# Decay attention and sticky mixture of experts: early outputs scaled on GpSimd, and a new order beside the early tiles

## The chip, the cores and the metric

One core of a Trainium2 chip runs the whole kernel. The metric is the device time of one execution in microseconds. TensorE does the matmuls, VectorE and ScalarE take results out of PSUM, GpSimd (POOL) splits weights and issues the indirect transfers, and SyncE (SP) issues all the other transfers. Each engine works off its own instructions in the order in which they were written; engines wait for each other through semaphores.

## The reference

The first half is causal attention with a decay, for 8 batches of 8 heads, 576 positions and 64 columns a head. Its output, with the heads side by side, is `x` with 512 columns a token. The second half is a mixture of 8 experts in which a token may keep the expert of the token before it:

```python
logits = np.einsum('bsd,de->bse', x, w_gate)
local_gate = 1.0 / (1.0 + np.exp(-np.einsum('bsd,de->bse', x, w_local).squeeze(-1)))
...
            fresh_e = int(np.argmax(logits[b, s]))
            if s == 0 or local_gate[b, s] < 0.5:
                e = fresh_e
            else:
                e = prev_e if prev_e >= 0 else fresh_e
...
            h = np.maximum(x[b, s] @ w1[e], 0.0)
            out[b, s] = p[e] * (h @ w2[e])
```

`p` is the softmax of the token's logits, so each output row is multiplied by one probability. `w1[e]` is 512 by 1024 and `w2[e]` 1024 by 512.

## The kernel before

Attention runs batch by batch. All values that matter are kept as a high and a low float16 part, so that a product is three matmuls (high by high, high by low, low by high). The tokens go to DRAM (`xs`), to be gathered by expert later.

Routing (`route`, L1352) is done for pairs of batches, four times. It has a critical part (`crit`: `mxs`, `fresh`, `gated`, `rows`, ... `place`, `place2`, `slot`, `marks`, `invert`, `invert2`) that finds each token's slot, and a part that isn't needed at once (`rest`: `prob`, `prob2`, `prob3`, `prob4`, `pmarks`, `pinvert`, `pinvert2`) that brings the probabilities into the same slots. Most steps are small VectorE operations. Some are small matmuls into `psG`, a pool of one PSUM bank (L1797), so the next such matmul may be issued only when the last result has been read.

After the third pair, the tokens of the first six batches are known. So three tiles of 128 tokens each, for experts 0 and 1, can be computed at once (`both_early`, L1994), while the last two batches are still being routed. Expert 0's weights `W0` and the first two of eight blocks of expert 1's (`PW`, `NP = 2`) are split into high and low by GpSimd; the other six blocks of expert 1 are split by `piece` (L2010): the high part by ScalarE (L1822), the low one by VectorE (L1826), and the load of a later block behind it.

`experts` (L1655) is a generator. In the first layer it takes eight chunks `fc` of 12 matmuls into `z` (two PSUM buffers). The relu of a chunk, a ScalarE instruction to `hh` and a VectorE one to `hl`, is issued after the matmuls of the next chunk. Then it takes three tiles of 24 matmuls into `y` (two buffers); `put` of a tile (L1671), a ScalarE copy to `o` that multiplies by the probability and a scatter by GpSimd, is issued after the matmuls of the next tile. For the early tiles, `experts` yields after every two matmuls: expert 0 has the steps 0 to 47 (first layer) and 48 to 83 (second), expert 1 the steps 84 to 131 and 132 to 167.

`run` (L1719) goes through these steps and calls what is due at each: `todo` and `at` are two lists, sorted by step. `AT` (L63) holds the steps of the last pair's critical routing; `beside(x, f)` (L1900) adds `f` at step x. This table alone decides what stands in an engine's line ahead of a relu. At the same step, functions are called in the order in which they were added.

What is added by name: `turn_xl` turns the last tokens of the last batch; `mult`, `half`, `add` (from `gate`) make the last batch's logits from `xt`; `close_attention` (L1848) frees attention's memory, opens the pools for expert 1's weights and starts their loads; `late_tok` (L1873) gathers expert 0's late tokens and `next_tokens` (L1876) expert 1's (`x1l`), each gather being followed by a transpose on SyncE, with three buffers `xg`; `totals`, `ranks`, `numbers`, `rank_loads` prepare the other experts, which are taken in the order of their load; `early_probs` gives the probabilities of the early tiles.

Then `fixed` (L2133) computes the late tiles of experts 0 and 1, and `ranked` those of the other six.

Of the kernel before, what the change touches and what calls it, by code (L numbers as in the profile page):

```python
# [59 lines left out]
HB = (1, 1)  # L60
ST = 4
XP = 20
AT = (6, 15, 18, 30, 30, 36, 44, 49, 62)  # L63

T0 = 9700.0
DUE = (("k2", 11000), ("q2", 12500), ("k3", 14500), ("q3", 15500), ("v", 18000), ("v4", 20500), ("a", 26000), ("b", 29000))
# [6 lines left out]
def kernel(  # L73
# [1116 lines left out]
    def whole(fn):  # L1190

        for _ in fn() or ():
            pass
# [91 lines left out]
    def rtile(shape, dt, name):  # L1285
        return rt.tile(shape, dt, name=name)
# [65 lines left out]
    def route(g, last):  # L1352
# [4 lines left out]
        OH = OHA[:, g]  # L1357
        R = {}
        NV = nc.vector
        aux, AUX = (nc.gpsimd, POOL) if big is nc.gpsimd else (NV, None)  # L1360

        def mxs():
            R["mx"] = rtile([128, GC], F32, "mx")
            R["kp"] = rtile([128, 2, GC], F16, "kp")
            NV.tensor_reduce(R["mx"], Lx, axis=AX.X, op=ALU.max)
            yield
            NV.scalar_tensor_tensor(R["kp"], Lg[:, :, E].unsqueeze(1).broadcast_to([128, 2, GC]), ZTHR, notfirst,
                                    ALU.is_gt, ALU.mult)
            R["mxb"] = R["mx"].unsqueeze(2).broadcast_to([128, GC, E])
# [110 lines left out]
            aux.tensor_tensor(hm, t128[:, gs], ov, ALU.add)  # L1480

        def marks():
            HI = R["HI"] = rtile([128, GC, NM], F16, "HI")
            RH = R["RH"] = rtile([128, GC, 2, NM], F16, "RH")
            LO = R["LO"] = rtile([128, GC, 128], F16, "LO")
            NV.tensor_tensor(HI, imain.unsqueeze(1).broadcast_to([128, GC, NM]),
                              R["hm"].unsqueeze(2).broadcast_to([128, GC, NM]), ALU.is_equal)
            yield 320 if big is NV else 1480
            if big is NV:
                NV.tensor_scalar(RH[:, :, 0], HI, irow[:, 0:1], None, ALU.mult)  # L1490
                yield 250
                NV.tensor_scalar(RH[:, 4::5, 0], HI[:, 4::5], irow[:, 1:2], None, ALU.mult)
                yield 2060
            else:
                big.tensor_scalar(RH[:, :, 0], HI, irow[:, 0:1], 1.0, ALU.mult, ALU.mult)
                big.tensor_scalar(RH[:, 4::5, 0], HI[:, 4::5], irow[:, 1:2], 1.0, ALU.mult, ALU.mult)
            big.tensor_tensor(RH[:, :, 1], HI, icol[:, gs].unsqueeze(2).broadcast_to([128, GC, NM]), ALU.mult)
            NV.tensor_tensor(LO, i128.unsqueeze(1).broadcast_to([128, GC, 128]),
                              lo[:, gs].unsqueeze(2).broadcast_to([128, GC, 128]), ALU.is_equal)
# [145 lines left out]
    def tokens(pool, xT, cols, n, rows=NT, half=False):  # L1645
# [6 lines left out]
            nc.sync.dma_start_transpose(out=xT[:, :, i * 128:i * 128 + m], in_=xg[0:m])  # L1652
        return xT

    def experts(W, xT, n, prob, scat, hp, op, width=704, every=6, half=None):  # L1655

        wh, wl, uh, ul = W
# [11 lines left out]
            nc.vector.scalar_tensor_tensor(lv, z[:, 0:nh, 0:wd], 0.0, hv, ALU.max, ALU.subtract)  # L1669

        def put(t, y):  # L1671
            o = op.tile([128, DM], F32, name="o", bufs=2 if op is ep else 3)
            nc.scalar.activation(o, y, AF.Copy, scale=prob(t))  # L1673
            nc.gpsimd.indirect_dma_start(out=outf, out_offset=bass.IndirectOffsetOnAxis(ap=scat(t), axis=0), in_=o,  # L1674
                                         in_offset=None, bounds_check=NT - 1, oob_is_err=False)
# [172 lines left out]
    def close_attention():  # L1848
# [3 lines left out]
        EX["wpb"] = ctx.enter_context(tc.tile_pool(name="wpb", bufs=1))  # L1852
        EX["W"] = wtiles(EX["wpb"])
        stage2 = EX["stage"] = ctx.enter_context(tc.tile_pool(name="stage2", bufs=ST))

        first = early_weights(stage2, EX["W"], range(NP), 1)
        for _, f in first[0:2]:
# [18 lines left out]
    def next_tokens(cols, n2, rows=NT):  # L1876
        return tokens(EX["xp"], EX["xp"].tile([128, 8, 704], F16, name="xT"), cols, n2 // 2, rows, bool(n2 % 2))
# [12 lines left out]
    def both(*fs):  # L1890
        return lambda: [whole(f) for f in fs]
# [1 line left out]


    last = gate(B - 1)
    todo = [turn_xl, lambda: whole(last[0]), both(*last[1:], close_attention, *crit[0:3]), both(*crit[3:6]), both(*crit[6:8]), both(*crit[8:10]),
            both(*crit[10:13]), both(*crit[13:17]), both(*crit[17:19], all_idx, late_tok)]
    at = list(AT)

    def beside(x, *fs):  # L1900

        at.append(x)
        todo.append(both(*fs))
# [107 lines left out]
        NW.pop(0)()  # L2011

    for i in range(4 * NP):
        beside(19 + 3 * i, lambda: EX["PW"].pop(0)())
    REST = EX["rest"]
    for x, f in zip((0, 1, 2, 3, 4, 34, 35), REST, strict=True):
        beside(x, f)
    beside(36, early_probs)
    beside(19, open_ranks)
    beside(64, lambda: EX.update(x1l=next_tokens(lambda i: EX["ga"][:, CAP + EARLY + i:CAP + EARLY + i + 1], CAP2[1] - 2 * EARLY)))  # L2020
    for i in range(16 - 2 * NP):
        beside(65 + 24 * i // (16 - 2 * NP), piece)
    for i, f in enumerate((totals, ranks, numbers, rank_loads, gathers, *rest, all_probs, scatters, half_tiles, caps)):
        beside((63, 63, 64, 95, 96)[i] if i < 5 else 92 + 6 * (i - 5), f)
    seq = sorted(range(len(at)), key=lambda x: at[x])
    run(both_early(), [todo[x] for x in seq], [at[x] for x in seq], 400)
    pump(0)
    sidx, xp_, wpb = EX["sa"], EX["xp"], EX["wpb"]
    ectx.close()

# [223 lines left out]
```

## Time and profile before

| | |
|---|---|
| median of 3 runs | 891.14 us (891.06 to 893.96) |
| the profiled execution | 888.74 us, span 887.0 us |
| mean granted TensorE clock | 0.964 |
| TensorE busy | 784.8 us, 88% |
| VectorE busy | 525.2 us, 59% |
| ScalarE busy | 433.3 us, 49% |
| GpSimd busy | 404.9 us, 46% |
| attention's last matmuls | near 434.8 us |
| early tiles | 434.9 to 531.6 us |

In the rows of the timeline, the first number is the start in us from the span's start, the second the duration of the group, then engine, line, operation, output and inputs, shapes and count. What stands in brackets at the end is how long the engine sat idle just before, and what ended that. A row with "x2" or "x3" stands for instructions back to back. `PEclk` in the tables of stretches is the granted clock of TensorE as a share of its full speed.

### The profile page before, as it was taken

What the parts mean: (1) busy time and instruction counts of PE and PEld (TensorE: products, weight loads), DVE (VectorE), ACT (ScalarE), POOL (GpSimd) and SP (SyncE); (2) the same over time, 40 slices, a digit from 0 to 9 for tenths busy, and PEclk for the clock granted to TensorE, in tenths of its full rate; (3) what the DMA queues carried; (4) which work ended last, traced back from release to release, by engine and by line L of the source; (5) the groups of instructions that cost most, each with busy time, mean ns of one, the idle gap of its engine ahead of it and who ended that gap; (6) DMA issues with size and microseconds to landing.
All of it is one profiled execution on the core that took longest, in us unless ns stands there. A gap on an engine that the chain in (4) does not pass through costs nothing. (4 is left out here: it accounts for less than half of the span.)

```text
span 887.0 us, 20948 instructions
## 1 busy us (share of the span) xinstructions
PE 784.8 (88%) x8438; PEld 542.5 (61%) x8438; DVE 525.2 (59%) x1120; ACT 433.3 (49%) x804; POOL 404.9 (46%) x473
## 2 busy tenths in 40 slices
PE   5776999889997898969769498999999999999993
PEld 3655778667876787757534256575564847575541
DVE  8765878888878877888857331534073634434110
ACT  4764778758876687748413111534142424323110
POOL 9595768487854969236981200321311212121100
PEclk9988999999999999989979799999999999999997
DMA  6979979586974868079472800657354654735000
GB/s 164 190 132 222 180 166 171 118 172 142 156 171 83 159 137 164 4 157 216 100 264 60 272 24 25 153 184 204 113 146 164 151 176 147 193 123 143 37 16 29
DMA packets 205588, 124.81 MB, mean 141 GB/s; under 512 B 145612, under 2 KB 181582, under 8 KB 205404
## 3 DMA queue, kind: packets, MB, share of 16 engines
q1 hardware_dynamic: 199345, 104.04, 51.4%
q0 software_dynamic: 6144, 19.41, 6.7%
q8 instruction: 67, 1.10, 0.5%
q14 instruction: 32, 0.26, 0.1%
HBM read 72.41 MB, written 19.62 MB: 104 GB/s over the span
## 5 line engine op out<-in xcount | busy, mean ns | idle before, releaser
L1682 PE MATMUL z<-xT,wh 128*128 128x288 f16 (+4 forms) x960 | 186.0, 305 | 26.9 <-DVE hl L1669 26.9
L910 ACT ACTIVATE P<-st,nm 128x512 f32<-128x512 f32 (+3 forms) x288 | 152.4, 585 | 39.7 <-DVE nm L890 35.5
L890 DVE TENSOR_REDUCE nm<-st 128x1 f32<-128x512 f32 (+4 forms) x264 | 134.5, 544 | 28.5 <-PE st L886 17.4
L1669 DVE SCALAR_TENSOR_TENSOR hl<-z,hh 128x576 f16<-128x576 f32 (+5 forms) x80 | 52.7, 663 | 164.7 <-ACT hh L1668 164.5
L930 ACT CAST ph<-pt 128x512 f16<-128x512 f32 (+1 forms) x200 | 115.7, 582 | 55.4 <-PE pt L925 54.0
L925 PE MATMUL pt<-ident,P 128*128 128x128 f32 x784 | 125.0, 284 | 14.9 <-DVE pl L934 7.9
L1682 PEld LDWEIGHTS <-wh 128*128 128x128 f16 x960 | 94.0, 99 | 68.8 <-issue 20.0
L934 DVE TENSOR_TENSOR pl<-pt,ph 128x512 f16<-128x512 f32 x168 | 111.8, 669 | 27.6 <-ACT ph L930 25.5
L1682 PE MATMUL z<-xT,wl 128*128 128x288 f16 (+4 forms) x480 | 120.2, 305 | 0.0
L1704 PE MATMUL y<-ul,hh 128*128 128x512 f16 x288 | 109.2, 379 | 0.0
L1704 PE MATMUL y<-uh,hl 128*128 128x512 f16 x288 | 109.2, 379 | 0.0
L1704 PE MATMUL y<-uh,hh 128*128 128x512 f16 x288 | 109.1, 379 | 0.0
L1668 ACT ACTIVATE hh<-z 128x576 f16<-128x576 f32 (+5 forms) x80 | 45.9, 575 | 124.4 <-PE z L1682 121.2
L925 PEld LDWEIGHTS pt<-ident,P 128*128 128x128 f32 x784 | 85.9, 144 | 32.4 <-issue 9.7
L1704 PEld LDWEIGHTS <-hh 128*128 128x128 f16 x576 | 56.2, 98 | 65.6
L904 PE MATMUL xp<-VH,pl 128*128 128x65 f16 (+1 forms) x960 | 91.6, 195 | 4.3 <-DVE pl L934 4.3
L1674 POOL DMA_INDIRECT out_dram<-o,ranki x26 | 27.3, 1049 | 147.4 <-ACT o L1673 116.8
L904 PE MATMUL xp<-VH,ph 128*128 128x65 f16 (+1 forms) x960 | 93.5, 197 | 0.9 <-ACT ph L930 0.9
L904 PE MATMUL xp<-VL,ph 128*128 128x65 f16 (+1 forms) x960 | 92.4, 195 | 0.0
L879 PE MATMUL st<-KB,QB 70*128 70x256 f16 (+4 forms) x448 | 80.4, 290 | 13.1 <-DMA KB<-Ak 8.5
L904 PEld LDWEIGHTS <-ph 128*128 128x128 f16 (+1 forms) x1920 | 84.1, 103 | 8.7 <-issue 3.3
L879 PE MATMUL st<-Ak,Aq 128*128 128x256 f16 (+4 forms) x448 | 80.9, 293 | 7.6 <-ACT P L910 7.2
(378 smaller groups left out, 1295.5 us busy)
## 6 DMA issues: line engine op xcount, KB each, us to landing
stg<-in_moe_w_dram SPq DMA_DIRECT2D x64, 512.0 KB
xs<-xr SPq DMA_DIRECT2D x16, 512.0 KB
ldq<-in_q_dram SPq DMA_DIRECT2D x14, 512.0 KB
ldk<-in_k_dram SPq DMA_DIRECT2D x14, 512.0 KB
ldv<-in_v_dram SPq DMA_DIRECT2D x28, 256.0 KB
KB<-Ak SPq DMA_DIRECT2D x14, 256.0 KB
QB<-Aq SPq DMA_DIRECT2D x13, 256.0 KB
ldv<-in_v_dram SPq DMA_DIRECT2D x20, 64.0 KB
```

The costliest lines, as they stand in the source:

```text
L879: nc.tensor.matmul(st[p0:p0 + m, co:co + n], lhsT=queries(lq, kk, h, c), rhs=rhs, start=(ps == 0 and first and co == col), stop=(ps == 1), ...
L890: nc.vector.tensor_reduce(dst, src, axis=AX.X, op=ALU.max, negate=True)
L904: nc.tensor.matmul(xo, lhsT=a[:, c0:c0 + m], rhs=w[:, vi, :], start=False, stop=(i == n - 1 and jj == 2), skip_group_check=True)
L910: nc.scalar.activation(P[:, c0:c1].rearrange("p (k x r) -> p k r x", r=2, x=64), st[:, c0:c1].rearrange("p (k r x) -> p k r x", r=2, x=64) ...
L925: nc.tensor.matmul(U["pt"][:, i * 128:(i + 1) * 128], lhsT=P[:, i * 128:(i + 1) * 128], rhs=ident, is_transpose=True, start=(i == 0), stop ...
L930: nc.scalar.copy(U["ph"][:, :cols], U["pt"][:, :cols])
L934: nc.vector.tensor_tensor(U["pl"][:, :cols], U["pt"][:, :cols], U["ph"][:, :cols], ALU.subtract)
L1668: nc.scalar.activation(hv, z[:, 0:nh, 0:wd], AF.Relu)
L1669: nc.vector.scalar_tensor_tensor(lv, z[:, 0:nh, 0:wd], 0.0, hv, ALU.max, ALU.subtract)
L1674: nc.gpsimd.indirect_dma_start(out=outf, out_offset=bass.IndirectOffsetOnAxis(ap=scat(t), axis=0), in_=o, in_offset=None, bounds_check=NT ...
L1682: nc.tensor.matmul(z[:, a, 0:wd], lhsT=w[:, d, fc * 128:(fc + 1) * 128], rhs=xT[:, x, a * wd:(a + 1) * wd], start=(i == 0), stop=(i == len ...
L1704: nc.tensor.matmul(y, lhsT=a[:, fc, t * 128:(t + 1) * 128], rhs=u[:, fc], start=(i == 0), stop=(i == len(prods) - 1))
```

## The change

The early tiles' outputs are no longer multiplied by ScalarE. `put` copies `y` to `o` as it is, into a pool of three buffers of its own (`oe`), and notes the tile in a list. `scaled`, called at the steps 118, 122, 126 and 158 and twice at the end, takes the oldest tile, multiplies it on GpSimd in place by its probability and issues its scatter.

```diff
-AT = (6, 15, 18, 30, 30, 36, 44, 49, 62)
+AT = (7, 26, 26, 31, 37, 42, 42, 50, 54, 58, 71)
...
+        def own(name):
+            return name + "l" * (g == B // 2 - 1)
...
+    unscaled = []
+
+    def scaled():
+
+        o, prob, scat, t = unscaled.pop(0)
+        nc.gpsimd.tensor_scalar(o, o, prob(t), 1.0, ALU.mult, ALU.mult)
+        nc.gpsimd.indirect_dma_start(out=outf, out_offset=bass.IndirectOffsetOnAxis(ap=scat(t), axis=0), in_=o,
+                                     in_offset=None, bounds_check=NT - 1, oob_is_err=False)
...
-            o = op.tile([128, DM], F32, name="o", bufs=2 if op is ep else 3)
+            o = (EX["oe"] if op is ep else op).tile([128, DM], F32, name="o", bufs=3)
+            if op is ep:
+
+                nc.scalar.activation(o, y, AF.Copy)
+                unscaled.append((o, prob, scat, t))
+                return
...
-    todo = [turn_xl, lambda: whole(last[0]), both(*last[1:], close_attention, *crit[0:3]), both(*crit[3:6]), both(*crit[6:8]), both(*crit[8:10]),
+    todo = [turn_xl, lambda: whole(last[0]), both(*last[1:], close_attention, crit[0]), both(crit[1]), both(crit[2]), both(*crit[3:6]), both(*crit[6:8]), both(*crit[8:10]),
...
-        beside(19 + 3 * i, lambda: EX["PW"].pop(0)())
+        beside(27 + 3 * i, lambda: EX["PW"].pop(0)())
...
-    for x, f in zip((0, 1, 2, 3, 4, 34, 35), REST, strict=True):
+    for x, f in zip((75, 79, 86, 92, 98, 112, 114), REST, strict=True):
...
-    beside(36, early_probs)
-    beside(19, open_ranks)
-    beside(64, lambda: EX.update(x1l=next_tokens(lambda i: EX["ga"][:, CAP + EARLY + i:CAP + EARLY + i + 1], CAP2[1] - 2 * EARLY)))
+    beside(116, early_probs)
+    for x in (118, 122, 126, 158):
+        beside(x, scaled)
+    beside(28, open_ranks)
+    beside(123, lambda: EX.update(x1l=next_tokens(lambda i: EX["ga"][:, CAP + EARLY + i:CAP + EARLY + i + 1], CAP2[1] - 2 * EARLY)))
...
-        beside(65 + 24 * i // (16 - 2 * NP), piece)
+        beside(60 + i if i < 4 else 85 + 4 * (i - 4), piece)
...
-        beside((63, 63, 64, 95, 96)[i] if i < 5 else 92 + 6 * (i - 5), f)
+        beside((72, 73, 74, 121, 122)[i] if i < 5 else 124 + 4 * (i - 5), f)
...
     pump(0)
+    while unscaled:
+        scaled()
```

The third pair's probabilities (`REST`) move from the first steps of expert 0 to the second layer of expert 0 and the first of expert 1. The last pair's critical routing starts 11 steps later by its first matmuls (26 instead of 15) and is cut into more pieces; its tiles `mx`, `HI` and `LO` get names of their own (`own`), since the third pair's are now read after them. The gathers of expert 1's late tokens move from step 64 to 123. The first four of expert 1's pieces move from 65 to 71 to the steps 60 to 63, the other eight from 73 to 87 to 85 to 113. The late steps of the last pair's probabilities move from 92 and following to 124 and following.

VectorE at the start of the early tiles, before. `xl` is the last attention output, `ex` to `rp` are the third pair's probabilities, `hl` the relus:

```order
L285 TENSOR_TENSOR xl<-xnl,xl 128x256
L1514 TENSOR_TENSOR ex<-L,mx 128x80
L1523 TENSOR_REDUCE den<-ex 128x10
...
L1538 CAST pp<-pe 128x10
L1549 TENSOR_TENSOR rp<-HI,pp 128x10x48 x3
L1887 CAST xlt<-psG 128x512
L1669 SCALAR_TENSOR_TENSOR hl<-z,hh 128x384 x2
```

The same place with the change:

```order
L285 TENSOR_TENSOR xl<-xnl,xl 128x256
L1906 CAST xlt<-psG 128x512
L1682 SCALAR_TENSOR_TENSOR hl<-z,hh 128x384 x3
L2240 MEMSET ctr 128x1
L838 TENSOR_TENSOR L<-psG,half 128x36
L838 TENSOR_TENSOR L<-psG,half 64x9
L1369 TENSOR_REDUCE mxl<-L 128x10
L1371 SCALAR_TENSOR_TENSOR kp<-L,notfirst 128x20
L1682 SCALAR_TENSOR_TENSOR hl<-z,hh 128x384
```

The probabilities are gone from here, three relus come before the gate's logits (`L`), and a fourth behind the first two routing operations.

VectorE at the end of the last pair's marks, before. `LO` is the last of the marks, `invi` reads the result of `invert` out of `psG`:

```order
L1497 TENSOR_TENSOR RH<-HI,icol 128x10x48
L1498 TENSOR_TENSOR LO<-i_176,lo 128x1280
L1508 TENSOR_TENSOR invi<-psG,invi 128x96
L1587 SCALAR_TENSOR_TENSOR mt<-invi 128x48
L1588 TENSOR_SCALAR mgf<-mt 128x48
```

With the change:

```order
L1501 TENSOR_TENSOR RH<-HIl,icol 128x10x48
L1502 TENSOR_TENSOR LOl<-i_176,lo 128x1280
L1844 SCALAR_TENSOR_TENSOR wl<-stg,wh 128x1024 x2
L1512 TENSOR_TENSOR invi<-psG,invi 128x96
L1591 SCALAR_TENSOR_TENSOR mt<-invi 128x48
```

Two low parts of expert 1's weights now stand between the marks and `invi`.

GpSimd behind the last split of expert 1's weights, before. `mg` are the indices of the late tokens, `xs` those of the early outputs' rows, `xp` their probabilities:

```order
L314 TENSOR_TENSOR wl<-stg,wh 128x512 x2
L1650 DMA xg<-xs,mg 128x1024 x4
L1650 DMA xg<-xs,mg 64x1024
L1674 DMA out_dram<-o,xs 4608x512 x6
```

With the change:

```order
L314 TENSOR_TENSOR wl<-stg,wh 128x512 x2
L1654 DMA xg<-xs,mg 128x1024 x2
L1664 TENSOR_SCALAR o<-o,xp 128x512
L1665 DMA out_dram<-o,xs 4608x512
...
L1654 DMA xg<-xs,mg 128x1024 x2
L1654 DMA xg<-xs,mg 64x1024
L1664 TENSOR_SCALAR o<-o,xp 128x512
L1665 DMA out_dram<-o,xs 4608x512
```

Two gathers (expert 0's late tokens) stay first; two multiplies with their scatters come next, then the three gathers of expert 1's late tokens, and then the other four multiplies with theirs.

More of the change, by code (lines that the diff above doesn't have):

```diff
@@ L1359, in route @@
         NV = nc.vector
+        def own(name):
+            return name + "l" * (g == B // 2 - 1)
         aux, AUX = (nc.gpsimd, POOL) if big is nc.gpsimd else (NV, None)
         def mxs():
-            R["mx"] = rtile([128, GC], F32, "mx")
+            R["mx"] = rtile([128, GC], F32, own("mx"))
             R["kp"] = rtile([128, 2, GC], F16, "kp")
@@ L1482, in marks @@
         def marks():
-            HI = R["HI"] = rtile([128, GC, NM], F16, "HI")
+            HI = R["HI"] = rtile([128, GC, NM], F16, own("HI"))
             RH = R["RH"] = rtile([128, GC, 2, NM], F16, "RH")
-            LO = R["LO"] = rtile([128, GC, 128], F16, "LO")
+            LO = R["LO"] = rtile([128, GC, 128], F16, own("LO"))
             NV.tensor_tensor(HI, imain.unsqueeze(1).broadcast_to([128, GC, NM]),
@@ L1854, in close_attention @@
         stage2 = EX["stage"] = ctx.enter_context(tc.tile_pool(name="stage2", bufs=ST))
+        EX["oe"] = ectx.enter_context(tc.tile_pool(name="oe", bufs=3))
         first = early_weights(stage2, EX["W"], range(NP), 1)
```

## The prediction

> **What bounds the kernel now.** I read the profile's grouped instructions first. TensorE is busy 88% of the span, and its one large wait has a row of its own:
>
> ```profile
> L1682 PE MATMUL z<-xT,wh 128*128 128x288 f16 (+4 forms) x960 | 186.0, 305 | 26.9 <-DVE hl L1669 26.9
> ```
>
> 26.9 us of TensorE idle time, all for `hl`, the second half of a relu on VectorE. The timeline of TensorE shows where, with the idle time and its releaser in brackets, and the first matmul of the early tiles of expert 0 (434.92), of expert 1 (486.65), and of the late tiles (531.65):
>
> ```profile
> 434.92 0.50 PE L1682 MATMUL z<-xT,wh 128*128 128x384 f16 x2
> 447.69 0.82 PE L1682 MATMUL z<-xT,wh 128*128 128x384 f16 x2 [8.47 <-DVE hl L1669]
> 457.25 0.50 PE L1682 MATMUL z<-xT,wh 128*128 128x384 f16 x2 [2.81 <-DVE hl L1669]
> 462.73 0.16 PE L1403 MATMUL psG<-ident,sc 10*1 10x10 f16 x1 [1.04 <-DVE crow L1410]
> 486.65 0.49 PE L1682 MATMUL z<-xT,wh 128*128 128x384 f16 x2
> 502.03 0.80 PE L1682 MATMUL z<-xT,wh 128*128 128x384 f16 x2 [11.32 <-DVE hl L1669]
> 531.65 0.38 PE L1682 MATMUL z<-xT,wh 128*128 128x256 f16 x2
> 536.70 0.38 PE L1682 MATMUL z<-xT,wh 128*128 128x256 f16 x2 [2.27 <-DVE hl L1669]
> ```
>
> So the stage of the early tiles takes 531.65 - 434.92 = 96.73 us. Every one of these waits has the same form: two z buffers, so chunk fc+2 needs the relu of chunk fc, and that relu stands in line on VectorE or ScalarE behind something else. VectorE's rows name the first:
>
> ```profile
> 436.85 0.64 DVE L1514 TENSOR_TENSOR ex<-L,mx 128x80 f32<-128x80 f32 x1
> 446.49 0.68 DVE L1887 CAST xlt<-psG 128x512 f16<-128x512 f32 x1
> 447.09 1.01 DVE L1669 SCALAR_TENSOR_TENSOR hl<-z,hh 128x384 f16<-128x384 f32 x2
> ```
>
> The third pair's probabilities occupy VectorE from 436.85 to 446.49, and the relus come after them. For the second, ScalarE, GpSimd and SyncE's queue:
>
> ```profile
> 476.55 2.94 ACT L1822 ACTIVATE uh<-stg 128x1024 f16<-128x1024 f32 x3
> 493.30 0.69 ACT L1673 ACTIVATE o<-y,xp 128x512 f32<-128x512 f32 x1 [10.94 <-DMA out_dram<-o,xs]
> 499.04 1.06 ACT L1822 ACTIVATE uh<-stg 128x1024 f16<-128x1024 f32 x1 [5.06 <-DMA stg<-in_moe_w_dram]
> 535.81 0.66 ACT L1668 ACTIVATE hh<-z 128x256 f16<-128x256 f32 x2 [3.22 <-DMA out_dram<-o,xs]
> ```
>
> ```profile
> 463.62 2.27 POOL L314 TENSOR_TENSOR wl<-stg,wh 128x512 f16<-128x512 f32 x2
> 479.10 1.05 POOL L1650 DMA_INDIRECT xg<-xs,mg  x1 [13.21 <-DVE tot L1934]
> 487.84 0.96 POOL L1650 DMA_INDIRECT xg<-xs,mg  x1 [4.16 <-DMA xT<-xg]
> 490.34 1.02 POOL L1674 DMA_INDIRECT out_dram<-o,xs  x1 [0.30 <-issue]
> ```
>
> ```profile
> 482.59 11.71 SPq L1652 DMA_TRANSPOSE xT<-xg  x5
> 494.39 0.54 SPq L1835 DMA_DIRECT2D stg<-in_moe_w_dram  x1
> ```
>
> The third early output needs one of two `o` buffers, so it waits (10.94) for the first output's scatter, which GpSimd issues at 490.34 behind five gathers, two of which wait for transposes. After it, ScalarE waits for the last weight block of expert 1 (5.06), whose load SyncE issues at 494.39 behind the same five transposes. Only then comes the relu. Two causes stand one behind the other.
>
> **The change part by part.** The plain matmul work is the same before and after. Its pitch is read from a stretch without waits:
>
> ```profile
> 505.74 0.49 PE L1682 MATMUL z<-xT,wh 128*128 128x384 f16 x2
> 512.56 0.79 PE L1555 MATMUL psG<-rp,LO 128*128 128x144 f16 x10
> 516.11 0.38 PE L1704 MATMUL y<-uh,hh 128*128 128x512 f16 x1
> ```
>
> 42 first-layer matmuls lie between the first two rows: 6.82 / 42 = 0.1624 us. 72 second-layer matmuls lie between 516.11 and 531.65: 0.2158 us. The stage has 192 and 144 of them: 31.2 + 31.1 = 62.3 us. Of the other 34.4 us the waits above (without the last) are 8.47 + 2.81 + 1.04 + 11.32 = 23.6. A third part is the clock; the table of stretches shows TensorE's busy time in the third column and the granted clock third from the end:
>
> ```profile
> 447.70:451.11 3.41, 3.41 (x26) 1.88 (x27) 0.40 (x1) 0.00 (x0) 3.25 (x4) 0.51 0.92 314
> 454.53:457.94 3.41, 0.69 (x4) 0.41 (x5) 3.06 (x6) 0.44 (x1) 3.06 (x4) 0.99 0.96 356
> 457.94:461.35 3.41, 3.41 (x12) 1.42 (x11) 0.00 (x0) 0.00 (x0) 3.26 (x3) 0.51 1.00 389
> ```
>
> After the stops at 447.69 and 457.25 matmuls run 3.4 us at half clock, losing 1.7 each; 12 matmuls from 502.03 to 505.74 take 3.71 instead of 1.95, 1.8 more. That is 5.2. The remaining 5.6 is routing's small matmuls and waits under 0.6, which I keep.
>
> Removed: third-pair probabilities no longer precede the first relu, so 8.47 goes. What is next there is `xlt` (0.68) and a relu (0.5), against 1.95 us of matmuls in a chunk: a stop of about 0.1. The 11.32 goes with both its causes: three `o` buffers hold expert 0's three outputs, the copy needs neither the probability nor a scatter, and block 7's load now stands ahead of all late transposes on SyncE. It waits only for GpSimd's split of block 0, about 461. The half clock (5.2) goes with the stops. The 2.81 shrinks: the seven routing operations that stood ahead of one relu now stand ahead of three. I take 1.2, bounds 0 and 2.81. The 1.04 stays, since the two hops are still issued together. The gate's products now come at step 26, near 444.0; `xt`'s transposes are issued by 441.7, and no row shows their landing: I take 0, bounds 0 and 2. The 2.27 goes: the first late `hh` waited for the last scatter (535.81), whose buffer is now in another pool that this `hh` doesn't follow. If it still did, the multiply would add 0.7 to it.
>
> Added, routing under GpSimd's splits. Routing runs about 10 us earlier in absolute time, while GpSimd still splits weights until 463.62 + 2.27 = 465.9, as before. Minimum, median and maximum of the operations concerned, in ns; each maximum belongs to a pass with GpSimd at work, each minimum to the one near 473 with GpSimd idle:
>
> ```profile
> L1452 DVE TENSOR_TENSOR EX<-IN,OHA x2: 199/557/915, 376.3 to 470.5; 128x80 f16<-128x80 f16 x2
> L1454 DVE TENSOR_TENSOR EX<-EX,cnt x2: 242/503/764, 377.7 to 470.7; 128x80 f16<-128x80 f16 x2
> L1486 DVE TENSOR_TENSOR HI<-imain,hm x4: 659/1468/1482, 184.5 to 473.5; 128x480 f16<-128x480 f16 x4
> L1490 DVE TENSOR_SCALAR RH<-HI,irow x2: 345/734/1123, 385.2 to 474.2; 128x480 f16<-128x480 f16 x2
> ```
>
> `EX` twice costs 0.72 + 0.52 more, with 0.2 of slack before `place` at step 58: a stop of 1.0, bounds 0 and 1.2. `HI` and `RH` cost 0.8 + 0.8 more, and two small ones by their likeness 0.9. I take place at about 460, so they fall under the splits; later ones do not.
>
> The Trainium skill, in "SBUF — State Buffer", section "SBUF: two separate sides", says that GpSimd and a VectorE operation with two SBUF inputs or in a two-port mode exclude each other for a whole instruction. The rows agree: these are such operations. By the rule alone, each of the ten such operations could lose a full GpSimd instruction of 1.1 us, an estimate of 11 instead of my 3.7; the rows decide.
>
> The chain from `place` to `invert`, and what stands behind it:
>
> ```profile
> 472.00 0.23 DVE L1465 TENSOR_TENSOR pm<-psG,OHA 128x80 f32<-128x80 f32 x1
> 475.30 1.49 DVE L1498 TENSOR_TENSOR LO<-i,lo 128x1280 f16<-128x1280 f16 x1
> 477.68 0.26 DVE L1508 TENSOR_TENSOR invi<-psG,invi 128x96 f32<-128x96 f32 x1 [0.90 <-PE psG L1504]
> 480.47 2.38 DVE L1826 SCALAR_TENSOR_TENSOR wl<-stg,wh 128x1024 f16<-128x1024 f32 x2
> 506.93 0.16 DVE L1535 TENSOR_TENSOR pe<-pe,den 128x10 f32<-128x10 f32 x1
> 508.93 1.78 DVE L1549 TENSOR_TENSOR rp<-HI,pp 128x480 f16<-128x480 f16 x3
> ```
>
> From 472.00 to 476.79 the marks take 4.79; with 2.5 more, 7.3, against 13 steps x 0.432 = 5.6 on TensorE: a stop of 1.7 at `invert`, bounds 0 and 2.5. Then two `wl` (2.38) now stand ahead of `invi` (0.26), and the one routing bank of PSUM must be read before `totals` can write it, with 0.43 + 0.43 us of TensorE work between: a stop of 1.8, bounds 1.3 and 1.8.
>
> Expert 1's first layer now shares VectorE with the third pair's probabilities. ScalarE gives `uh` of block 4 only after expert 0's last output (0.69 + 0.98), VectorE follows with `ul` (1.19), the pieces of `pe` and `pp` (506.93 to 508.93 without one relu: 1.5) and the relu (0.5): some 5.4 us after the expert's start, where TensorE wants the third chunk at 24 x 0.1624 = 3.9. Stop 1.4, bounds 0 and 2. Then `ul`, `rp` and a relu, 1.19 + 1.78 + 0.5 = 3.5 against 1.95: 1.5, bounds 0 and 2. After that a relu and one `ul` (1.7) fit.
>
> The multiplies: GpSimd's nearest row is a scalar multiply of almost this size:
>
> ```profile
> L1495 POOL TENSOR_SCALAR RH<-HI,irow x2: 664/664/665, 189.3 to 291.3; 128x480 f16<-128x480 f16 x2
> ```
>
> Six at 0.7, each followed by its scatter (1.0). Queued behind the first two are the three gathers of expert 1's late tokens. They need `early_probs` (about 490 by this walk), so gathers end near 498 and transposes near 508 (five took 11.7 before). The tokens are wanted after expert 0's late tiles, which begin near 512 and whose second layer alone is 48 x 0.2158 = 10.4. Cover at least 14 us, so I cost multiplies, scatters and gathers at nothing. Without it, each us late is a us.
>
> Sum: new stops 0.1 + 1.2 + 1.04 + 1.0 + 1.7 + 1.8 + 1.4 + 1.5 = 9.7; the stage takes 62.3 + 5.6 + 9.7 = 77.6 instead of 96.7, that is 19.1 less, with the 2.27 behind it 21.4. Later waits and all work after are untouched. The profiled execution took 888.74 (span 887.0): 867.3. The median of the runs is 2.4 higher, 891.14: 869.7. I give 868.5.
>
> **The rivals.**
> (a) More of it comes back. The clock gate closes again: a stretch with TensorE busy 0.69 of 3.41 was followed by half clock. The stops at `invert` and `totals`, 3.5 us within 4.4, could empty such a stretch; three gated ones cost 1.7 each, and with every stop and the `xt` wait at its upper bound (5.7 more) the time is about 879. For it: several stops lie close together. Against: none fills a stretch alone.
> (b) No change. Moving expert 1's late gathers behind the multiplies makes their tokens late: 891. For it: the first multiply waits for `early_probs`, and GpSimd waits in order. Against: the cover of 14 us and then the 21 gained must be used up.
> (c) Slower. Stops keep TensorE's share low in stretch after stretch, and the clock stays at half through both experts. Each gated stretch costs 1.7, so 13 eat the gain and 16 make it slower by over 0.5%; all 22 give about 905, less the stops that half speed hides, some 8: 897. It decides by the share: 0.69 of 3.41 gated, and the largest idle share of mine is about that only once. "TensorE: Matmul & The Clock Gate" of the Trainium skill, Part 1, states a free-running window of about 3.4 us with an idle window halving the clock. The trace agrees with the length: both half-clock rows last 3.41; by that rule alone no stop of mine would gate anything and the time stays 868.5, since none is 3.4 long. It differs on the condition: 0.69 of the stretch was busy and the clock fell all the same, so the row decides.
> (d) It doesn't do what it says: the first late `hh` or the third `o` still waits for a scatter. That costs 3 to 11: 872 to 880, much the same as (a).
>
> **How the numbers follow.** The forecast has 0.76, (a) with (d) 0.14, (b) 0.06, (c) 0.04. The low end leaves out the contention (1.0 + 1.7) and half of expert 1's stops (1.5) and stands on the profiled execution: 867.3 - 4.2 = 863, rounded to 862.5. The high end reaches to (a)'s 879. Half a per cent, 4.5 us, is about what a measurement of this kernel can tell from no change: faster 0.90, same 0.06, slower 0.04.
>
> **What would show it.** Right: TensorE's waits for `hl` fall from 26.9 to about 7, none over 3; the late tiles begin near 512; ScalarE shows no wait for `out_dram`; a stop of nearly 2 us stands at `totals`. Wrong: a wait of over 5 us anywhere between 435 and 515, half clock over more than two stretches there, or a wait of the late tiles for `xT`.

## The result, and the profile with the change

The change makes the kernel 2.4% faster: 870.62 us, median of 4 runs (869.35 to 872.1), beside 891.83 us (891.06 to 893.96, 4 runs) of the kernel before. The ratio is 0.9758, 95% interval 0.9738 to 0.9778. The prediction was 868.5 in a range of 862.5 to 879.0. The profiled execution took 871.77 us, span 870.1.

The grouped instructions first. The row of the first layer's matmuls ends with the idle time before them, which was 26.9 us:

```profile
L1700 PE MATMUL z<-xT,wh 128*128 128x288 f16 (+4 forms) x960 | 182.6, 301 | 5.3 <-DVE hl L1682 5.3
```

The timeline of TensorE, with the first matmul of the early tiles, every stop over 0.4 us, and the first matmul of the late tiles:

```profile
440.93 0.82 PE L1700 MATMUL z<-xT,wh 128*128 128x384 f16 x2
...
454.31 0.50 PE L1700 MATMUL z<-xT,wh 128*128 128x384 f16 x2 [1.37 <-DVE hl L1682]
456.88 0.48 PE L1700 MATMUL z<-xT,wh 128*128 128x384 f16 x2 [0.44 <-DVE hl L1682]
461.01 0.16 PE L1407 MATMUL psG<-ident,sc 10*1 10x10 f16 x1 [1.21 <-DVE crow L1414]
466.67 0.18 PE L1439 MATMUL psG<-idc,so 10*128 10x10 f16 x1 [0.54 <-DVE so L1434]
476.18 0.17 PE L1950 MATMUL psG<-cnt,ones 128*128 128x8 f16 x1 [0.85 <-DVE invi L1512]
486.01 0.48 PE L1700 MATMUL z<-xT,wh 128*128 128x384 f16 x2 [0.99 <-DVE hl L1682]
489.31 0.49 PE L1700 MATMUL z<-xT,wh 128*128 128x384 f16 x2 [1.20 <-DVE hl L1682]
516.08 0.38 PE L1700 MATMUL z<-xT,wh 128*128 128x256 f16 x2
```

The stage takes 516.08 - 440.93 = 75.15 us instead of 96.73. Its seven stops sum to 6.6; none is over 1.4. What lies behind the first late matmul takes 354.0 instead of 355.3 (870.1 - 516.08, 887.0 - 531.65), because the late tiles' stop of 2.27 is gone and one of 0.65 is new (at 752.72). But attention itself ended 6.0 us later in this execution (first early matmul at 440.93 instead of 434.92). So the two profiled spans differ by 21.6 + 1.3 - 6.0 = 16.9 only, while the medians differ by 21.2. The second traces, below, show that the end of attention varies from execution to execution for one and the same program.

ScalarE shows what became of the third output and of the first late `hh`:

```profile
481.15 0.60 ACT L1688 ACTIVATE o<-y 128x512 f32<-128x512 f32 x1 [1.45 <-PE y L1722]
481.64 1.99 ACT L1840 ACTIVATE uh<-stg 128x1024 f16<-128x1024 f32 x2
...
517.59 0.38 ACT L1681 ACTIVATE hh<-z 128x256 f16<-128x256 f32 x1 [0.66 <-PE z L1700]
```

The third output waits for TensorE and no longer for a scatter, the weight parts behind it wait for no load, and the first late relu waits for its own matmuls. No row of ScalarE in the stage waits for `out_dram`. The table of stretches shows two of the emptier ones; the granted clock stands third from the end:

```profile
453.87:457.28 3.41, 2.52 (x15) 1.45 (x16) 3.34 (x6) 0.49 (x1) 3.33 (x5) 1.00 0.89 328
474.33:477.74 3.41, 2.56 (x22) 1.33 (x21) 3.20 (x13) 0.00 (x0) 0.45 (x1) 1.00 0.00 0
```

From 442.0 to 858 the clock is full: the half clock of before, which cost 5.2 us, has gone with the long stops. Only the first 1.1 us of the stage, 440.93 to 442.0, still ran at half clock, left over from the end of attention; that costs about 0.5 and is seen in the 0.82 of the first row above, which is 0.50 in the second trace below.

### The profile page after: what moved, and what is told of

Its sections match the earlier page's. It is cut to its first block, busy times and chain, and to the rows that moved or that the text cites. A ratio compares the mean times of both kernels' runs of the same rounds, so it can differ in the third digit from the quotient of the medians.

```text
span 870.1 us, 20950 instructions
## 1 busy us (share of the span) xinstructions
PE 785.2 (90%) x8438; PEld 544.6 (63%) x8438; DVE 527.6 (61%) x1120; ACT 432.8 (50%) x804; POOL 409.9 (47%) x479
## 5 line engine op out<-in xcount | busy, mean ns | idle before, releaser
L1700 PE MATMUL z<-xT,wh 128*128 128x288 f16 (+4 forms) x960 | 182.6, 301 | 5.3 <-DVE hl L1682 5.3
```

The costliest lines, as they stand in the source:

```text
L1700: nc.tensor.matmul(z[:, a, 0:wd], lhsT=w[:, d, fc * 128:(fc + 1) * 128], rhs=xT[:, x, a * wd:(a + 1) * wd], start=(i == 0), stop=(i == len ...
```

## The experiments

Medians, with the ratio to the kernel before on the same chip; "stage" is from the first early to the first late matmul in the run's own trace.

| run | median us (range) | ratio, 95% interval | stage us |
|---|---|---|---|
| e1 probabilities late, old order | 883.08 (882.39 to 885.1) | 0.9899 (0.9874 to 0.9925) | 93.30 |
| e2 new order, three `o` | 874.78 (871.2 to 876.5) | 0.9815 (0.9785 to 0.9846) | 81.63 |
| e3 new order, two `o` | 880.08 (878.15 to 882.19) | 0.9863 (0.9829 to 0.9896) | 89.78 |
| e4 block 7 behind the transposes | 879.7 (877.11 to 883.08) | 0.9865 (0.9825 to 0.9904) | 89.01 |
| r0 the change again | 869.22 (868.5 to 871.17) | 0.9757 (0.973 to 0.9785) | 75.11 |
| e5 pieces behind `totals` | 869.34 (866.63 to 870.64) | 0.9753 (0.9724 to 0.9781) | 74.08 |
| e6 four multiplies | 869.0 (865.7 to 872.41) | 0.975 (0.9719 to 0.9781) | 75.44 |
| e7 splits longer | 872.93 (871.49 to 874.4) | 0.979 (0.9763 to 0.9817) | 79.89 |
| e8 load earlier | 868.87 (868.25 to 870.72) | 0.9754 (0.9727 to 0.9781) | 73.69 |
| e9 combined | 867.84 (866.79 to 868.78) | 0.9733 (0.9706 to 0.9761) | 72.94 |
| e10 the kernel before again | 894.48 (one run) | | 94.01 |
| e11 smoothed | 865.76 (863.28 to 868.01) | 0.9713 (0.9686 to 0.9741) | 72.07 |

### One part alone: the probabilities (e1)

Everything that the probabilities need is as in the change (`REST`, `early_probs`, `scaled`, the pool `oe`, the last pair's probabilities from 124); the tables of the order are those of before, with expert 1's late tokens at 64 and the routing in its old pieces:

```diff
-AT = (7, 26, 26, 31, 37, 42, 42, 50, 54, 58, 71)
+AT = (6, 15, 18, 30, 30, 36, 44, 49, 62)
...
-        beside(60 + i if i < 4 else 85 + 4 * (i - 4), piece)
+        beside(65 + 24 * i // (16 - 2 * NP), piece)
```

> Only the probabilities move: the third pair's late steps, the multiplies on GpSimd and the three buffers of `o` as in the change; the routing's steps, expert 1's pieces and its late tokens as before. My theory: the first stop (8.47), the half clock behind it (1.7) and the late tiles' 2.27 go, but the stop at expert 1's third chunk stays at about 11, since block 7's load still stands behind five transposes: 891.8 - 12.4 = 879.4, plus up to 2.7 for operations that now run under GpSimd's splits: 879 to 883. Rival (the third `o` was what held ScalarE): the 11.32 goes as well, 866 to 870.

Measured: 883.08, 8.2 less than before, just past the slow edge of what was expected. TensorE's stops and the ScalarE instruction ahead of the last one:

```profile
463.04 0.20 PE L1465 MATMUL psG<-EX,ones 128*128 128x80 f16 x1 [2.00 <-DVE EX L1458]
471.39 0.60 PE L1508 MATMUL psG<-RH,LOl 128*128 128x96 f16 x10 [2.54 <-DVE LOl L1502]
498.14 0.80 PE L1700 MATMUL z<-xT,wh 128*128 128x384 f16 x2 [11.39 <-DVE hl L1682]
```

```profile
493.77 1.06 ACT L1840 ACTIVATE uh<-stg 128x1024 f16<-128x1024 f32 x1 [10.30 <-DMA stg<-in_moe_w_dram]
```

The stop at the start is gone and the one at expert 1's third chunk is as long as before, although no output waits for a scatter any more: the wait is now 10.30 for block 7's load. The rival falls. `place` (2.00) and `invert` (2.54) cost 4.5 between them, more than the 2.7 that was expected: from `place` to the first mark takes 5.0 (463.04 to 468.04), in r0 below, with GpSimd done, 1.7 (466.73 to 468.46). The stop at `invert` was followed by half clock, 472.7 to 476.1. The old order also asks for the gate's products so early that TensorE waits 0.60 and 0.82 for the transposes of `xt`, and half clock follows there too, 445.4 to 448.8. In the change these products come at 450.56 and wait for nothing.

### One part alone: the order (e2, e3)

The order is that of the change; `REST` is back at steps 0 to 4, 34 and 35, `early_probs` at 36, and ScalarE multiplies. e2 keeps the pool of three `o`, e3 has the two of before:

```diff
-            if op is ep:
-                nc.scalar.activation(o, y, AF.Copy)
-                unscaled.append((o, prob, scat, t))
-                return
...
-            o = (EX["oe"] if op is ep else op).tile([128, DM], F32, name="o", bufs=3)
+            o = op.tile([128, DM], F32, name="o", bufs=2 if op is ep else 3)
```

> Only the order moves: routing, pieces and expert 1's late tokens as in the change; the probabilities early and the multiply on ScalarE as before, but `o` with three buffers in the pool of its own. My theory: 8.47 and its half clock stay; the stop of 11.32 and its half clock (1.8) go, 2.81 shrinks by 1.6, the late tiles' 2.27 goes, `totals` costs 1: 891.8 - 16.8 = 875, 873 to 877. Rival (the parts stand one behind another, so that one alone gives nearly nothing): over 885.

> As the run with only the order moved, but `o` has its two buffers in the old pool. My theory: the third output finds a free buffer anyway, because with the late gathers gone from GpSimd's line the first scatter is issued at once, so only the 2.27 at the late tiles comes back: 2.3 more than with three buffers, 877 (875 to 880). Rival (the number of buffers decides): a stop of several us at expert 1's third chunk again, 885 to 889.

e2 took 874.78, inside 873 to 877. Its stage has the first stop unchanged, none at expert 1's third chunk, and the one at `totals`:

```profile
447.30 0.82 PE L1695 MATMUL z<-xT,wh 128*128 128x384 f16 x2 [8.48 <-DVE hl L1682]
...
479.62 0.17 PE L1945 MATMUL psG<-cnt,ones 128*128 128x8 f16 x1 [0.85 <-DVE invi L1512]
```

e3 took 880.08, 5.3 more than e2, just above the expectation and for a reason that it had excluded. GpSimd, ScalarE and TensorE of e3:

```profile
483.32 1.05 POOL L1654 DMA_INDIRECT xg<-xs,mg  x1 [14.10 <-DVE tot L1947]
...
485.94 1.03 POOL L1687 DMA_INDIRECT out_dram<-o,xs  x1 [0.30 <-issue]
```

```profile
489.60 0.69 ACT L1686 ACTIVATE o<-y,xp 128x512 f32<-128x512 f32 x1 [8.37 <-DMA out_dram<-o,xs]
...
526.91 0.66 ACT L1681 ACTIVATE hh<-z 128x256 f16<-128x256 f32 x2 [3.23 <-DMA out_dram<-o,xs]
```

```profile
493.20 0.49 PE L1695 MATMUL z<-xT,wh 128*128 128x384 f16 x2 [2.15 <-DVE hl L1682]
```

The two gathers that stay ahead wait 14.10 for the routing's last result, so the first scatter still goes out late and the third output still waits 8.37. Of that TensorE feels 2.15 at expert 1's third chunk, plus 2.28 at the late tiles, plus stretches of half clock. So two causes did stand one behind the other. In the new order, with the load out of the way, the scatter costs TensorE 2.15 at this place (5.3 in all by the medians, with the late tiles and the half clock). The load alone leaves the whole stop, 11.39 in e1.

### The load alone, put back (e4)

```diff
-    beside(123, lambda: EX.update(x1l=next_tokens(lambda i: EX["ga"][:, CAP + EARLY + i:CAP + EARLY + i + 1], CAP2[1] - 2 * EARLY)))
+    beside(73, lambda: EX.update(x1l=next_tokens(lambda i: EX["ga"][:, CAP + EARLY + i:CAP + EARLY + i + 1], CAP2[1] - 2 * EARLY)))
...
-        beside(60 + i if i < 4 else 85 + 4 * (i - 4), piece)
+        beside(74 + 2 * i, piece)
```

> The change, with expert 1's late tokens at step 73 and the twelve pieces at 74, 76 and so on, so that block 7's load stands behind five transposes again; probabilities, multiplies and `o` as in the change. My theory: first gather near 477, load about 17 us later as before, landing near 499, the third chunk of expert 1 near 501 instead of 487: a stop of 14 to 16 there, 883 to 887. Rival (the scatter and the buffers were the cause): no new stop, 869 to 873.

SyncE's queue and TensorE:

```profile
477.17 10.51 SPq L1656 DMA_TRANSPOSE xT<-xg  x5
487.77 0.54 SPq L1853 DMA_DIRECT2D stg<-in_moe_w_dram  x1
```

```profile
463.88 0.20 PE L1465 MATMUL psG<-EX,ones 128*128 128x80 f16 x1 [2.55 <-DVE EX L1458]
493.55 0.80 PE L1700 MATMUL z<-xT,wh 128*128 128x384 f16 x2 [12.57 <-DVE hl L1682]
```

The stop is back, 12.57 instead of the expected 14 to 16, and with it the stage is 13.9 longer than the change's. Not all of that is the load's: the 2.55 at `place` and the half clock behind it (465.1 to 468.5) go with the early end of attention in this trace, 435.82. The time, 879.7, is less than the 883 that I expected at least; beside the 869.22 and 870.62 of the change, the load costs about 10. Why the stop is shorter than expected was not followed. The rival (no new stop) falls.

### The change again, and the kernel before again (r0, e10)

Both unaltered.

> The change once more, unaltered, for a second trace. In its first trace attention's last matmul lies near 440.9, in those of four kernels with the same attention at 433.0 to 435.9, while GpSimd's splits end at 467 in all. My theory: the early end of attention is the usual one and the late one chance; with an end near 436 the last pair's prefix and marks fall under the splits, `place` stops for about 2.5 and `invert` for up to 2.5, so the earlier start is given back: stage 78 to 81 instead of 75.15, time 868 to 872. Rival (a late end belongs to this kernel): first early matmul near 441 again, stage 75, no stops at `place` and `invert`.

> The kernel before, unaltered, for a second trace. In its first one attention ends with the first early matmul at 434.92, in five traces of the changed kernel and its near variants at 438.9 to 440.9. Theory: this belongs to the program, so 433 to 436 again, beside 438 and more in the other two of this call. Rival (it goes with the chip that a call runs on): 438 or more here as well, or 433 to 436 in all three.

TensorE of the change's second trace:

```profile
438.90 0.50 PE L1700 MATMUL z<-xT,wh 128*128 128x384 f16 x2
...
466.73 0.20 PE L1465 MATMUL psG<-EX,ones 128*128 128x80 f16 x1 [1.68 <-DVE EX L1458]
...
514.01 0.38 PE L1700 MATMUL z<-xT,wh 128*128 128x256 f16 x2
```

And of the second trace of the kernel before:

```profile
441.61 0.81 PE L1682 MATMUL z<-xT,wh 128*128 128x384 f16 x2
450.71 0.82 PE L1682 MATMUL z<-xT,wh 128*128 128x384 f16 x2 [4.49 <-DVE hl L1669]
...
505.08 0.80 PE L1682 MATMUL z<-xT,wh 128*128 128x384 f16 x2 [11.43 <-DVE hl L1669]
...
535.62 0.38 PE L1682 MATMUL z<-xT,wh 128*128 128x256 f16 x2
```

The kernel before ended attention at 441.61 this time, 6.7 later than in its first trace. So the late end does not belong to the changed program, and both theories on it fall. The chip alone doesn't settle it: e6 and e9, run beside e10 on the same chip, ended attention at 436.71 and 439.54. But the chip may have a part in it: the five traces from one chip (e1 to e4 and e11) begin the early tiles at 433.0 to 435.9, the seven from the other (r0 and e5 to e10) at 436.7 to 441.6. No run separates the chip from the program here, and what makes the end vary was not followed. Of r0's expectation the time and the contention at `place` came (1.68), not the early end of attention, the stop at `invert` or the longer stage. Over the two traces of each kernel the stage is 20.2 us shorter (95.4 to 75.1).

The second trace of before also shows that the stop of 8.47 was not all work. One tiny operation of the third pair's probabilities, in the first trace of before and in the second:

```profile
438.73 1.13 DVE L1527 TENSOR_SCALAR den<-den 128x10 f32<-128x10 f32 x1
```

```profile
445.75 0.17 DVE L1527 TENSOR_SCALAR den<-den 128x10 f32<-128x10 f32 x1
```

The chain from `ex` to `rp` took 9.7 us (436.85 to 446.57) with GpSimd splitting beside it, and 6.1 (443.46 to 449.58) when most of it fell into a time in which GpSimd waited for a load (445.7 to 450.0). The stop was 8.47 in the one and 4.49 in the other.

### GpSimd's splits, longer and earlier (e7, e8)

e7 does the last half of the last split four more times; e8 issues the load of expert 0's block 6 behind the split of block 3:

```diff
-        EX["PW"] = [f for _, f in first[2:]]
+        EX["PW"] = [f for _, f in first[2:]] + [first[-1][1]] * 4
...
-    for i in range(4 * NP):
+    for i in range(4 * NP + 4):
```

```diff
-                    queue.extend(early_weights(stage, W0, range(6)))
+                    first_six, last_two = (early_weights(stage, W0, r) for r in (range(6), range(6, 8)))
+                    first_six.insert(22, last_two.pop(0))
+                    queue.extend(first_six)
...
-    queue.extend(early_weights(stage, W0, range(6, 8)))
+    queue.extend(last_two)
```

> The change, with the last half of GpSimd's last split done four more times over (4.5 us more, ending near 472 instead of 467; same values). It prices VectorE's operations under GpSimd. My theory: the marks `HI` and `RH` and the small operations ahead of them take 2 to 2.5 us more, `invert` stops for 2 to 3 more: 2 to 4 slower than the change run beside it (a gated stretch of 1.7 included). Rival (GpSimd's work costs VectorE nothing at this place): within 0.7 of it.

> The change, with the load of expert 0's block 6 issued behind the split of block 3 instead of at the end of attention, so that GpSimd doesn't wait for it (4.07 in the change's trace) and its splits end near 463. My theory: `place` and `invert` stop for less: 2 to 4 us faster than the change run beside it, if attention ends near 436 there; nothing gained if it ends near 441. Rival (GpSimd's work costs VectorE nothing): within 0.7 of it either way.

e7 is 3.7 slower than r0 beside it (the ranges don't overlap). `place` stops for 2.76 instead of 1.68, `invert` and `totals` for these:

```profile
475.39 0.60 PE L1508 MATMUL psG<-RH,LOl 128*128 128x96 f16 x10 [0.61 <-DVE LOl L1502]
477.82 0.17 PE L1950 MATMUL psG<-cnt,ones 128*128 128x8 f16 x1 [1.40 <-DVE invi L1512]
```

And the stretch behind them runs at half clock:

```profile
474.33:477.74 3.41, 1.48 (x15) 0.64 (x13) 3.41 (x4) 0.00 (x0) 0.00 (x0) 0.99 0.00 0
477.74:481.15 3.41, 3.33 (x10) 1.19 (x9) 2.72 (x17) 0.55 (x2) 1.92 (x2) 0.51 0.15 30
```

So GpSimd's work does cost VectorE time here. The size came as expected, the place did not: the marks `HI` and `RH` took 0.66 and 0.34, as without GpSimd, and the operations ahead of them were held up (`EX` 1.07 and 1.24, `cnt` 1.13, `t` 0.72). The price of one operation is seen in `prefix`: r0, with GpSimd at work, and then e9 (which has e8's earlier load), with GpSimd done at 463.2:

```profile
464.10 1.30 DVE L1454 TENSOR_TENSOR_SCAN IN<-carry,OHA 128x80 f16<-128x80 f16 x1
465.43 0.97 DVE L1456 TENSOR_TENSOR EX<-IN,OHA 128x80 f16<-128x80 f16 x1
```

```profile
464.69 0.32 DVE L1454 TENSOR_TENSOR_SCAN IN<-carry,OHA 128x80 f16<-128x80 f16 x1
465.05 0.20 DVE L1456 TENSOR_TENSOR EX<-IN,OHA 128x80 f16<-128x80 f16 x1
```

e8 itself misses its expectation of 2 to 4: the stop at `place` is gone and the stage is 1.4 shorter than r0's, but 868.87 beside 869.22 is no difference that these runs can tell. Without its wait for the load GpSimd meets other operations instead: `kp`, `eq` and `G` take 0.68 + 0.92 + 0.81 where r0 has 0.18 + 0.72 + 0.39, and two stops ahead of a relu follow them, 0.88 and 0.56, where r0 has 0.38 and 0.37.

### The low parts behind `totals` (e5)

```diff
-        beside(60 + i if i < 4 else 85 + 4 * (i - 4), piece)
+        beside(74 + i if i < 4 else 85 + 4 * (i - 4), piece)
```

> The change, with the first four of expert 1's pieces at steps 74 to 77 instead of 60 to 63, so that no low part of the weights stands ahead of `invi`. My theory: the stop at `totals` (0.85) goes to nothing, 1 us less, and if the parts come late for expert 1's first matmuls, a stop of up to 1 there gives it back: -1 to +0.5 against the change run beside it. Rival (`totals` waits for the chain from `invert`, not for the low parts): the stop stays at 0.85.

The stop at `totals` is gone, nothing comes back at expert 1's start, and the stage is 1.03 shorter than r0's, as the low parts' theory has it. The medians, 869.34 and 869.22, cannot tell one microsecond.

### Four multiplies instead of one (e6)

```diff
         nc.gpsimd.tensor_scalar(o, o, prob(t), 1.0, ALU.mult, ALU.mult)
+        for _ in range(3):
+            nc.gpsimd.tensor_scalar(o, o, 1.0, 1.0, ALU.mult, ALU.mult)
```

> The change, with each output multiplied on GpSimd four times instead of once (three times by one, same values). It doubles and more the disputed cost: 2.1 us more a tile, 4.2 ahead of expert 1's late gathers, 12.4 in all. My theory (nobody waits for GpSimd there: the tokens' transposes end near 511 and are wanted near 537): 868 to 871, as the change. Rival (b) of the prediction (the late tokens come late): 4 to 12 slower, 873 to 882, with a wait of the late tiles for `xT`.

869.0, as the change. The last of expert 1's late gathers on GpSimd, and the next stop of TensorE:

```profile
503.45 1.18 POOL L1654 DMA_INDIRECT xg<-xs,mg  x1 [0.30 <-issue]
```

```profile
537.67 0.43 PE L1702 MATMUL z<-xT,wh 128*128 128x320 f16 x2 [1.26 <-DVE hl L1684]
```

The only stop there is the 1.26 for a relu that the kernel before has too; none is for `xT`. The multiplies cost nothing, even fourfold, and rival (b) of the prediction is excluded.

### What the traces point to (e9, e11)

e9 has e8's load, the pieces in the order in which ScalarE and VectorE have time for them, and the third pair's probabilities spread further. `early_probs`, `scaled`, the late tokens and the last pair's late steps mostly follow by 1 to 3 steps; of the diff, these lines:

```diff
-    for x, f in zip((75, 79, 86, 92, 98, 112, 114), REST, strict=True):
+    for x, f in zip((75, 79, 82, 86, 109, 116, 118), REST, strict=True):
...
-    for i in range(16 - 2 * NP):
-        beside(60 + i if i < 4 else 85 + 4 * (i - 4), piece)
+    for x, i in zip((60, 62, 66, 68, 74, 76, 97, 98, 103, 104, 115, 121), (0, 2, 4, 6, 1, 3, 5, 8, 7, 10, 9, 11), strict=True):
+        beside(x, lambda i=i: NW[i]())
...
```

> The change with what the traces point to: block 6 of expert 0 loaded earlier; the high parts of expert 1's blocks 2 to 5 in ScalarE's idle time before 477; the low parts of blocks 2 and 3 behind `totals`; the other low parts and the third pair's `rp` one behind each relu of expert 1's first layer. My theory: the stops of 1.68 at `place`, 0.85 at `totals` and 0.99 and 1.20 in expert 1 go, in all 4.7, and about 1 comes back in smaller ones: stage 71 to 72.5 instead of 75.1, time 865 to 866.5 where the change takes 869.2. Rival (the stops of the stage only move along, as they did with the earlier load): stage 74 to 75, 868 to 869.5.

867.84, more than the 865 to 866.5 expected. The four stops it aimed at are gone, but 0.59, 0.50 and 1.05 came up in expert 1, one because block 7's high part was asked for before its load had landed. e11 takes those apart, and the one of 1.56 at `ends`. In part, against e9:

```diff
-AT = (7, 26, 26, 31, 37, 42, 42, 50, 54, 58, 71)
+AT = (7, 26, 26, 31, 37, 42, 46, 50, 54, 58, 71)
...
-    for x, f in zip((75, 79, 82, 86, 109, 116, 118), REST, strict=True):
+    for x, f in zip((75, 79, 82, 86, 109, 116, 121), REST, strict=True):
...
```

> The combined kernel, with what is left of its stops taken apart: the matmul `ends` four steps behind `rows2` and `scan0` instead of at their step (stop of 1.56), block 7's high part at step 116 instead of 104, where it waited for its load (0.59), the third pair's `pinvert2` behind one more relu (0.50), the last pair's `gathers` and probabilities at 133 and later (1.05). My theory: 2.5 to 3.5 less than the combined kernel, stage 69.5 to 70.5, time 864.5 to 865.5. Rival (the chain of the last pair's routing sets the length of the stage, and the stops only move along): stage 72 to 73, 867 to 868.5.

```profile
435.27 0.50 PE L1700 MATMUL z<-xT,wh 128*128 128x384 f16 x2
...
463.60 0.20 PE L1465 MATMUL psG<-EX,ones 128*128 128x80 f16 x1 [2.55 <-DVE EX L1458]
...
507.34 0.38 PE L1700 MATMUL z<-xT,wh 128*128 128x256 f16 x2
```

865.76, against 864.5 to 865.5 expected, the lowest median of all. Expert 1 has no stop over 0.4 left. But attention ended early here, at 435.27, so `place` met GpSimd again and stopped for 2.55. Without that stop the stage would be about 69.5 instead of 72.07, an estimate. The intervals of e11 (0.9686 to 0.9741) and of the change (0.973 to 0.9785) still touch, so that e11 beats the change is likely and not settled; that it beats the kernel before is.

## Why the prediction was right, step by step

**What goes.** The first stop and its half clock, the stop at expert 1's third chunk and its half clock, and the late tiles' 2.27 are gone, as forecast: the sum said 19.1 in the stage and 2.27 behind it, 21.4 together, and the medians differ by 21.2. That these two agree so closely is in part luck, as the terms below show. Of the signs that were named, the waits for `hl` fell to 5.3 with none over 3, and in the stage ScalarE waits for no `out_dram`; `totals` stopped for 0.85 and not for nearly 2, and the late tiles began at 516.08 and 514.01 instead of 512, as attention ended later. e2 and e1 show that each half of the change carries its own part. "Two causes stand one behind the other" holds too: e1 takes the scatter away and leaves 11.39, e3 takes the load away and leaves a wait of 8.37 on ScalarE, of which TensorE feels 2.15. The cover that I gave the multiplies is real (e6).

**The base.** 67.9 us were forecast without the new stops; 75.15 - 6.60 = 68.6 in the first trace, with the 0.5 of half clock at its start in it, and 75.11 - 7.30 = 67.8 in the second.

**The new stops**, 9.7 forecast, 6.6 and 7.3 measured (`back` is the wait for the copy `so`):

| term | forecast | first trace | second trace |
|---|---|---|---|
| `xlt` | 0.1 | 0 | 0 |
| the relus beside the gate's logits | 1.2 | 1.37 + 0.44 | 0.38 + 0.37 |
| `rows` to `ends` | 1.04 | 1.21 | 1.40 |
| `back` | 0 | 0.54 | 0.43 |
| `place` | 1.0 | 0 | 1.68 |
| `invert` | 1.7 | 0 | 0 |
| `totals` | 1.8 | 0.85 | 0.85 |
| expert 1 | 1.4 + 1.5 | 0.99 + 1.20 | 1.00 + 1.19 |

The step that failed is "I take place at about 460, so they fall under the splits". `place` came at 468.7 in the first trace and 466.7 in the second, when the splits had just ended (467.6 and 466.3), so that the marks behind it ran alone: `HI` took 0.66 in both, the least that the rows of before show. The first trace:

```profile
465.38 2.26 POOL L314 TENSOR_TENSOR wl<-stg,wh 128x512 f16<-128x512 f32 x2
468.67 0.20 PE L1465 MATMUL psG<-EX,ones 128*128 128x80 f16 x1
470.40 0.66 DVE L1490 TENSOR_TENSOR HIl<-imain,hm 128x480 f16<-128x480 f16 x1
```

The later end of attention is only a part of that. `place` came 27.7, 27.8 and 28.1 us after the first early matmul (first trace, r0, e4), where 460 stands 25.1 after the 434.92 of the trace that was read. In e4, where attention ended at 435.82 and the routing is the change's, `place` came at 463.88, and the marks still ran alone:

```profile
464.95 2.27 POOL L314 TENSOR_TENSOR wl<-stg,wh 128x512 f16<-128x512 f32 x2
467.76 0.66 DVE L1490 TENSOR_TENSOR HIl<-imain,hm 128x480 f16<-128x480 f16 x1
```

So the stop of 1.7 at `invert` came in none of these three traces. The price of one operation was about right (`EX` 0.97 beside GpSimd and 0.20 without, 0.77 more where 0.72 was taken), but it was put in the wrong place. It fell on the operations ahead of the marks: the scan `IN`, which I had not counted, the first `EX`, and the copy `so`. What `place` pays depends on when attention ends: 0 with the first early matmul at 440.93, 1.67 to 1.68 at 439.55, 438.90 and 436.71 (e5, r0, e6), 2.55 at 435.82 (e4). In e1, where the old order brings the routing sooner, it is 2.00, and 2.54 at `invert`. `totals` was mis-sized by the same step, 0.85 for 1.8: as TensorE did not wait at `invert`, the two low parts had started (473.61) before `invert`'s matmuls (474.31), and I had put them behind.

**Rivals.** (a), the clock: in the change's two traces no stop of the stage was followed by half clock, but the mechanism is real. Half clock followed the stops of e7, three small ones in e3 (near 466, 494 and 528), and the 2.55 at `place` in e4 (465.1 to 468.5), whose routing is the change's. So where attention ends early, a part of (a) can come in the change too; two traces can't tell how often. (b) is excluded by e6. (c), half clock throughout, did not come: behind the first 1.1 us the stage has none in the first trace, and none at all in the second. That both half-clock rows of before last 3.41 was the width of the cut: the first half clock ran from 444.2 to 451.0, two such lengths, and half of it fell into the stop. (d) did not happen, by the ScalarE rows.

**Where the numbers stood.** The profiled execution of after is 4.5 above the 867.3 that the sum gives, with a stage 2.4 shorter than forecast, because attention took 6.0 longer in it and the work behind the stage 0.9 more than the sum has. The sum took the end of attention as fixed; it varies by more than any of the small terms.

## What to carry to other kernels

Where one stop has two waits one behind the other, removing the first alone may show nothing (in e1 the scatter's wait was gone and 11.39 remained); follow the chain past the first releaser and price what is late next. An operation's price under a busy GpSimd can be read from the trace, but whether it is paid depends on which of the two lines is late in that execution, so give such a term both ends of its range and expect it to move to the neighbours. A gain of 1 us in a stage is visible in its own trace long before the medians can tell it: measure the stage from its first to its last instruction and leave out what happens ahead of it.

## What was not expected of the hardware

- Half clock doesn't need an empty stretch, and TensorE's busy share alone doesn't decide it. The changes of the clock in one trace lie multiples of 3.413 us apart (the first and the last of before, at 24.35 and 505.63, are 141 of them apart). Cut into stretches at these instants, TensorE was busy 1.24 us ahead of half clock in e4, 1.57 in e7 (two stops of 0.61 and 1.40 close together) and 2.46 in e1; it was busy 1.40 in e11, 1.73 in r0 and 2.05 in the change, and the clock stayed full. What decides was not found.
- A scan of 128x80 takes 0.32 alone and 1.30 beside a GpSimd subtraction, and a `tensor_scalar` on 128x10, 0.17 and 1.13: both take about 1 us more, near the length of one GpSimd instruction (1.1), whatever the size of VectorE's. That agrees with what the Trainium skill says in "SBUF — State Buffer", section "SBUF: two separate sides", of a lock held for a whole instruction.
- The same program ended its attention at 434.92 and at 441.61 in two executions, 6.7 us apart; the times of these two differ by 5.7 us (888.74 and 894.48).
- ScalarE copies 128x512 from PSUM in 0.60 without a column of scales and in 0.69 with one.
